# Attention and MLP kernel: a new order of the work, b1 turned on TensorE, w2 loaded in two parts

## The chip, the cores and the metric

The kernel runs on one NeuronCore of a Trainium2 chip. TensorE does the matmuls and writes to PSUM, VectorE and ScalarE do element-wise work, GpSimd and SyncE (SP) mostly issue DMAs; SP, ScalarE and GpSimd each have a DMA queue of their own. The engines run side by side, each takes its own list in order, and semaphores tie them. The metric is device time in microseconds (us); lower is better. In the profile PE is TensorE, PEld its weight load, DVE is VectorE, ACT is ScalarE, POOL is GpSimd.

## What is computed

```python
def _A_ref(x, wqkv, wo):          # S=2048, D=640, H=32 heads of 20, W=8, dil=2
    q, k, v = ...                 # x @ wqkv, split in heads
    idx = pos[:, None] - off[None, :]            # position minus 0, 2, .. 14
    logits = jnp.einsum("bhsd,bhswd->bhsw", q, kg) * scale   # masked where idx < 0
    attn = _softmax(logits, axis=-1)
    o = jnp.einsum("bhsw,bhswd->bhsd", attn, vg)
    return (...) @ wo

def _B_ref(x, w1, b1, w2, b2):    # F=1536
    h = _gelu(jnp.einsum("bsd,df->bsf", x, w1) + b1)
    return jnp.einsum("bsf,fd->bsd", h, w2) + b2

xn = _layernorm(x, axis=-1)
return x + _A_ref(xn, A_wqkv, A_wo) + _B_ref(xn, B_w1, B_b1, B_w2, B_b2)
```

Each position attends to eight positions, two apart, and an MLP stands beside the attention on the same normalised input. Data is bf16.

## The kernel before

The 2048 positions are cut in four chunks (n = 0 to 3) of 512, each of four blocks (bl) of 128. For a chunk the work is: statistics of x (`st`), rstd (`rs`, `rc`), normalised x (`xn`), its transpose into xnT (chunk 0: TensorE `tp` and copies `tc`; later chunks: DMA transposes `tc` on SP), projections to q, k, v held with features on the partitions (chunk 0 in pieces: matmuls `ga`, `gb`, `gd`, `ge`, `hj`, copies `gc`, `hc`; later `pj`, with copies `pc`), eight products q times shifted k on VectorE (`qk`), logits by TensorE (`lg`, four pieces wp = 0 to 3 for a chunk), max, subtract, exp, sum, reciprocal and weights (`m`, `mx`, `ex`, `ss`, `ri`, `at`), spread over the partitions by DMA (`xd` on SP, `xs` on ScalarE, `xw` both landed), eight weighted products with v (`av`), their sums (`ad`, `ot`). The MLP's first matmul is `f1` (12 tiles ft a chunk), its gelu on ScalarE `ge`. The output of a block is `o`: four steps over the gelu tiles with w2 and a fifth (`o..4`) over oT with wo, each matmul cut in "lo" (512 columns) and "hi" (128). Then come a copy (`oc`) and an accumulating DMA on GpSimd (`od`). A name is the kind followed by chunk and part: `lg23` is piece 3 of chunk 2, `f1010` is f1 of chunk 0, tile 10, `o104` the fifth step of chunk 1, block 0.

The order on TensorE, VectorE, ScalarE and SP is written out by hand: `ORDER` lists all pieces, and the program runs through it once, emitting each piece's instructions on its engines. So every engine's own order is the list cut down to its pieces. `make_plan` gives each piece its function; its costs and due times do not enter the built program.

Projections, f1 and the pieces of chunk 0 share four PSUM buffers (`acc`); a buffer is free again when ScalarE has copied it out (`hc`, `pc`, `ge`). The logits have one PSUM tile (tag L), which before the first chunk serves as target of ten idle matmuls; the output has one pair of banks (psO).

The logits matmuls sum over the 20 lanes of each head with a matrix of zeros and ones, 32 columns wide, so that four 32-column tiles of the array are in use, one for each block j:

```python
nc.tensor.matmul(L[j * H : (j + 1) * H, 2 * wp : 2 * wp + 2, :], lhsT=head_of[:],
                 rhs=prod[:, :, t, j * P : (j + 1) * P], ...)
```

The bias b1 (1536 numbers) is needed with features on the partitions, as b1T (128 x 12), the bias of every gelu. It is loaded as 12 rows of 128 into `b1_rt` (16 rows, zeroed by GpSimd at line 335) by SP at line 354, sixth in its queue; a DMA transpose at line 360 turns it into `b1_t`, and VectorE copies that to b1T (`b1`, line 589). Line 349 is the one x load on ScalarE's queue, line 364 (`ld`) loads w2.

Of the kernel before, what the change touches and what calls it, by code (L numbers as in the profile page):

```python
# [13 lines left out]
BF16 = mybir.dt.bfloat16  # L14
F32 = mybir.dt.float32
PE, VE, SE, DQ, GQ = "pe", "ve", "se", "dq", "gq"
# [46 lines left out]
S, D, F, H, W, DIL = 2048, 640, 1536, 32, 8, 2  # L63
P = 128
DH = D // H
PAD = (W - 1) * DIL
KT, FT = D // P, F // P
# [8 lines left out]
MW = 16  # L76
# [5 lines left out]


ORDER = """
pad01 pad02 st00a st00 sm rs00 me nm rc00 sq xn00a xn00b tp00a tp00b tc00a rs01 ga tc00b rc01 xn01 gb2 tp01 gb3
tc01a tc01b gb4 gd gc0 ge st03a hj101 gc4 st02a gc1 st02 hj100 st03 hc101 rs02 hj102 rs03 rc02 xn02 hj202 rc03 hc102
xn03 tp02 hc202 hj200 st10a tc02 st13a hc100 st13 tp03 hj201 tc03 st12a st11a hj112 st12 hc201 hj111 st10 hc200 st11
hj011 hc111 st21a st20a hc112 hj110 st22a hc011 st21 rs1 hj012 st20 hc110 hj010 st23a hc012 st22 hj211 rc1 hc010
st23 xn13 qk011 f101 hc211 tc13 hj212 pad11 qk031 xn10 f108 hc212 f102 b1 qk021 ge08 tc10 hj210 qk001 ge01 f100 xn11
qk020 f104 hc210 tc11 ge00 f105 qk010 ge02 xn12 f1010 qk030 ge04 tc12 f109 ge010 qk000 f1011 st33a ge011 ld lg00  # L90
st32a rs2 lg01 lg02 lg03 ge09 pj104 mk m0 pj114 ge05 mx0 pc104 pj102 pc114 st31a ex0 pj112 st30a rc2 st33 pj111 st32
pj101 ss0 pc111 pj110 pc101 ri0 pc112 pj103 pad12 xn22 st30 pj100 at0 pc102 tc22 pc103 pj113 st31 pc100 pc110 f103
pc113 qk110 f107 xd0 ge03 f110 qk131 xs0 f106 qk121 ge10 f113 qk101 pj121 ge13 xw0 ge06 f112 qk100 pc121 xn23 f115
qk120 ge12 tc23 f118 xn21 qk130 ge07 pj123 qk111 o020 xn20 tc21 o021 ge18 lg10 rs3 lg11 av030 pj122 tc20 av000 o022
pc122 lg12 av001 lg13 pj120 av011 o023 pc120 ge15 pj124 av031 f111 rc3 pc124 av021 pj210 xn32 pad21 pj202 tc32 av010
pc123 pc210 pj212 ge11 av020 pj211 pc212 pc202 ad00 pj214 xn33 pc211 pj213 tc33 xn31 pj200 pc213 ad01 pc214 pj224
tc31 pj203 ad02 pj220 pc203 pc224 pj204 pc220 xp0 f1110 pc204 ot0 pc200 pj223 m1 pj201 pc223 xb0 o024 mx1 pc201 xn30
qk220 pj221 oc02 tc30 ex1 o000 qk231 o001 o002 qk210 o003 ss1 o004 ri1 pj313 oc00 pc221 at1 od00 pj301 pc313 o010
qk221 xd1 pc301 pad22 pj310 qk200 o011 pc310 pj303 qk201 o012 pc303 qk211 xs1 o013 pj300 xw1 qk230 o014 xl lg20 oc01
lg21 av110 pc300 o030 lg22 ge110 av130 lg23 pj311 m2 xp1 o031 xb1 mx2 f119 av101 ex2 o032 f117 av100 pj312 pc311 ss2  # L100
f138 pc312 od02 ge17 pj302 av120 o033 pc302 av111 f114 ge19 pj314 ad10 f121 pc314 ge38 f116 ge21 ri2 pad31 f1210 xp2
av121 o034 ge210 xb2 av131 f1111 oc03 at2 pj304 ge111 pj321 ad11 pc304 pj322 pc321 xb3 ge16 pj222 ge14 qk310 pc322
od01 o100 xs2 od03 o101 ad12 o102 pj320 f128 ot1 f130 ge28 qk320 pc320 pj323 xd2 qk300 o103 o104 qk301 f129 oc10
qk331 pc323 o110 xw2 f126 qk321 o111 ge26 qk311 pc222 o112 pj324 qk330 f127 pc324 lg30 lg31 av211 o113 lg32 av230
o114 av220 lg33 oc11 f125 m3 od11 o120 ge25 av210 o121 o122 av231 o123 o124 mx3 f123 av221 oc12 od12 o130 av200 o131
ge23 od10 ge29 o132 ad21 ex3 o133 o134 ge27 ss3 f1211 f122 av201 f124 ge22 ad20 ge211 f131 ge30 oc13 f120 f132 ge20
ad22 ge24 f1310 f1311 ge310 ge31 ri3 o210 ge311 o211 at3 o212 ot2 xs3 xd3 o213 f134 o214 f135 oc21 pad32 od21 o220
xw3 ge35 o221 o222 av300 o223 o224 av320 f137 oc22 av310 od22 o230 av331 o231 o232 av301 o233 o234 av330 f136 av321
oc23 od23 o200 ad31 o201 ge32 ge34 f133 ge37 f139 ge33 av311 ge36 o202 ge39 o203 ad30 o204 o330 oc20 o310 ad32 od20
o300 od13 o301 o311 ot3 o312 o302 o303 o313 o304 o314 oc30 od30 o320 oc31 o321 od31 o322 o323 o324 o331 oc32 o332  # L110
od32 o333 o334 ohi oclo ochi
""".split()


def make_plan(fns, offsets={}):

    pl = Plan(offsets)
# [6 lines left out]
    def f(kind, *a):  # L124
        return lambda: fns[kind](*a)

    def turned(n, pair=None):
        if n:
            return [f"tc{n}{bl}" for bl in range(BPC)]
        every = ["tc00a", "tc00b", "tc01a", "tc01b", "tc02", "tc03"]  # L130
        return every if pair is None else every[4 * pair : 4 + 4 * pair]
# [5 lines left out]
            f"hc{which}1{g}" for g in range(len(COLS))  # L137
        ]

    pl.add("b1", VE, 0.1, -90, [], f("b1"), after=24.3)  # L140
    for n in range(NCH):
        base = n * PERIOD
        prev = base - PERIOD
# [51 lines left out]
        if n == 0:  # L195
# [11 lines left out]
            for which, buf, land in ((0, q, wq), (1, k, wk), (2, v, wv)):  # L207
                for pair in range(0 if which else 1, 2):
                    for g, (a, b) in enumerate(COLS):
                        ps = ("acc", "gp", which, pair, g)  # L210
                        nm = pl.add(f"hj{which}{pair}{g}", PE, 0.55 * (b - a), -50 + which // 2, turned(0, pair), f("gp", which, pair, a, b), [xnT, ps], land)
# [12 lines left out]
        L = ("L", n)  # L224
# [62 lines left out]
def kernel(  # L287
# [16 lines left out]
    nc = tc.nc  # L304
# [6 lines left out]
    consts = ctx.enter_context(tc.tile_pool(name="consts", bufs=1))  # L311
    wts = ctx.enter_context(tc.tile_pool(name="wts", bufs=1))
    psA = ctx.enter_context(tc.tile_pool(name="psA", bufs=4, space=bass.MemoryType.PSUM))
    psL = ctx.enter_context(tc.tile_pool(name="psL", bufs=1, space=bass.MemoryType.PSUM))
# [16 lines left out]
    w2_sb = wts.tile([P, FT, D], BF16, name="w2_sb")  # L331
    wo2 = wts.tile([P, KT, D], BF16, name="wo2")
    b1_rt = consts.tile([MW, P], BF16, name="b1_rt")
    b1_t = consts.tile([P, MW], BF16, name="b1_t")
    nc.gpsimd.memset(b1_rt[:], 0.0)
    b2bc = consts.tile([P, D], BF16, name="b2bc")
    wqkv_v = A_wqkv.rearrange("(t p) n -> p t n", p=P)
# [3 lines left out]
    def load_x(b0, b1):  # L341
        nc.sync.dma_start(x_sb[:, b0:b1, :], x_nb[:, b0:b1, :])  # L342

    def load_w(s):
        nc.sync.dma_start(wqkv[s][:], wqkv_v[:, :, s * D : (s + 1) * D])  # L345

    load_x(0, 1)
    nc.vector.memset(x_sb[:, 1, 0:16], 0.0)
    nc.scalar.dma_start(x_sb[:, 1, :], x_nb[:, 1, :])
    load_w(0)  # L350
    load_w(1)
    load_x(2, BPC)
    load_w(2)
    nc.sync.dma_start(b1_rt[0:FT, :], B_b1.rearrange("(t p) -> t p", p=P))  # L354
    load_x(BPC, 2 * BPC)
    load_x(2 * BPC, NCH * BPC)
    for c in range(2):
        cs = slice(c * F // 2, (c + 1) * F // 2)
        nc.sync.dma_start(w1_sb[:, :, cs], w1_v[:, :, cs])
    nc.sync.dma_start_transpose(b1_t[:], b1_rt[:])  # L360


    def do_ld():
        nc.sync.dma_start(w2_sb[:], B_w2.rearrange("(t p) n -> p t n", p=P))
        nc.sync.dma_start(wo2[:], A_wo.rearrange("(p t) n -> p t n", t=KT))
        nc.sync.dma_start(b2bc[:], b2_bcast)


    ident = consts.tile([P, P], BF16, name="ident")
# [10 lines left out]
    b1T = consts.tile([P, FT], F32, name="b1T")  # L380
# [15 lines left out]
    tiles = {}  # L396
# [179 lines left out]
    def do_qk(n, wp, i):  # L576
# [8 lines left out]
            op=ALU.mult,  # L585
        )

    def do_b1():
        nc.vector.tensor_copy(b1T[:], b1_t[:, 0:FT])

    def do_lg(n, wp):
        L = get(("L", n), lambda: psL.tile([P, W, P], F32, tag="L", name="L"))
# [172 lines left out]
    with tc.manual_schedule(engines=engines):  # L765

        ones = nc.const_aps.tensor(1.0, [P, CH], BF16)
        idle = psL.tile([P, W, P], F32, tag="L", name="idle")
        for _ in range(WARM):
            nc.tensor.matmul(idle[:, 0:BPC, :], lhsT=ones[:, 0:P], rhs=ones, start=True, stop=True)  # L770
        pieces = make_plan(fns).by
        assert sorted(ORDER) == sorted(pieces)
        for name in ORDER:
            pieces[name]["fn"]()
# [30 lines left out]
```

## Time and profile before

| | |
|---|---|
| median of 6 runs (lowest, highest) | 214.41 us (214.18, 215.57) |
| profiled execution | 214.09 us |
| its span, first to last instruction | 212.1 us |
| granted TensorE clock | 1.00 in all of the span's slices |
| TensorE matmul, VectorE, ScalarE busy | 97%, 82%, 53% |
| HBM read and written | 10.0 MB and 7.5 MB |

The page gives busy times by engine, the chain of work that ended last, groups of instructions by line, and DMA issues. Matmul durations overlap (a 512-column matmul is shown with 0.38 us, and the next starts 0.22 us after it), so TensorE's time is read from starts. In the timeline each row is start (us from the span's start), busy us, engine, line, operation, output and inputs, count, and in brackets the idle time before it and what ended it.

| row of the page | what it is |
|---|---|
| L697 hps 234 records, L507 pps 73 + 71 + 74, L728 lo 184 + 77 | the 512-column matmuls (some records are missing; weight loads are all there) |
| L602 L x320, 10.2 us busy | the logits |
| L708 hT x48, 31.2 us busy; 7 table loads there, 9.0 us | gelu |
| L581 x32 and L675 x32, 45.4 and 45.8 us | the products qk and av |

### The profile page before, as it was taken

To read this page: it belongs to the slowest core of one execution; us is meant where nothing else is said; L and a number is where in the kernel's file an instruction comes from. 1 tells how busy PE (TensorE), PEld (TensorE's weight loads), DVE (VectorE), ACT (ScalarE), POOL (GpSimd) and SP (SyncE) were. 2 spreads that over 40 slices of the span, in tenths; PEclk is the share of its full clock that TensorE was granted. 3 is DMA by queue.
4 is the path that set the end of the run, shared out by engine and by line. 5 is a ranking of instruction groups with operands and counts; after the bars stand their busy time and mean duration, and the time that the engine had idled before them with its cause. 6 is when DMAs were issued, how large, how long until landed. Compare 5 with 4: busy or idle time off the path is not lost.

```text
span 212.1 us, 3641 instructions
## 1 busy us (share of the span) xinstructions
PE 205.7 (97%) x1510; PEld 117.7 (56%) x1534; DVE 173.5 (82%) x178; ACT 112.7 (53%) x194; POOL 19.8 (9%) x37
## 2 busy tenths in 40 slices
PE   7999989999999999999999999999999999999994
PEld 2999636554465555555645554555554555555552
DVE  3588996889979999997899999969999819998001
ACT  5676797995866856551576452312287321341210
POOL 2000000000000002110120240101101011101120
PEclk9999999999999999999999999999999999999999
DMA  6999827928220173776653699701121381222053
GB/s 219 365 362 372 74 39 184 387 50 183 62 49 0 31 186 33 126 119 133 156 72 61 216 144 188 142 4 15 20 31 8 45 199 19 30 29 31 0 65 62
DMA packets 24104, 23.93 MB, mean 113 GB/s; under 512 B 9112, under 2 KB 21912, under 8 KB 24088
## 3 DMA queue, kind: packets, MB, share of 16 engines
q1 hardware_dynamic: 17064, 14.69, 26.5%
q0 software_dynamic: 4144, 4.92, 17.9%
q10 hardware_dynamic: 2880, 4.10, 6.4%
q8 instruction: 12, 0.20, 0.4%
q14 instruction: 4, 0.03, 0.1%
HBM read 10.00 MB, written 7.54 MB: 83 GB/s over the span
## 4 chain that ended last, share of the span: by engine, by line
PE 85%; DMA 6%; DVE 3%; SPq 2%; issue 1%; ACT 1%; ACTq 0%
PE lo L728 27%; PE hps L697 23%; PE pps L507 23%; PE hi L730 8%; DMA x_sb<-in_A_x_dram 6%; PE L L602 5%; DVE stats L407 2%; DVE prod L581 1%; SPq L345 1%; SPq L342 1%; ACT L708 1%; SPq L354 0%; ACT hT L708 0%; DVE mv L409 0%; DVE osb L758 0%
## 5 line engine op out<-in xcount | busy, mean ns | idle before, releaser
L697 PE MATMUL hps<-xnT,w_sb 128*128 128x512 bf16 x234 | 55.6, 379 | 1.1 <-ACT hT L708 0.7
L675 DVE TENSOR_TENSOR pv<-vT,ax 128x2560 bf16<-128x2560 bf16 x32 | 45.8, 1483 | 10.6 <-DMA ax<-attn 7.5
L728 PE MATMUL lo<-w_sb,hT 128*128 128x512 bf16 x184 | 52.9, 379 | 0.1
L581 DVE TENSOR_TENSOR prod<-qT,kT 128x2560 bf16<-128x2560 bf16 x32 | 45.4, 1484 | 0.8 <-ACT kT L566 0.8
L730 PE MATMUL hi<-w_sb,hT 128*128 128x128 bf16 x192 | 40.3, 219 | 0.5 <-issue 0.2
L708 ACT ACTIVATE hT<-hps,b1T 128x512 bf16<-128x512 f32 x48 | 31.2, 688 | 17.2 <-PE hps L697 15.2
L697 PEld LDWEIGHTS <-w_sb 128*128 128x128 bf16 x240 | 22.8, 98 | 27.1 <-issue 1.4
L684 DVE TENSOR_TENSOR pv<-pv 128x5120 bf16<-128x5120 bf16 x12 | 33.8, 2822 | 0.2
L735 ACT CAST osb<-lo 128x512 bf16<-128x512 f32 x15 | 8.8, 586 | 46.8 <-PE hi L730 25.5
L728 PEld LDWEIGHTS <-hT 128*128 128x128 bf16 x192 | 18.7, 98 | 22.4 <-issue 0.4
L741 POOL DMA_DIRECT2D out_dram<-osb x15 | 13.0, 866 | 103.3 <-ACT osb L736 87.7
L728 PE MATMUL lo<-wo,oT 128*128 128x512 bf16 x77 | 22.5, 379 | 0.0
L730 PEld LDWEIGHTS <-hT 128*128 128x128 bf16 x192 | 18.4, 98 | 2.8
L507 PE MATMUL pps<-xnT,wq_sb 128*128 128x512 bf16 x73 | 18.4, 379 | 0.1
L507 PE MATMUL pps<-xnT,wv_sb 128*128 128x512 bf16 x71 | 18.0, 380 | 0.2
L507 PE MATMUL pps<-xnT,wk_sb 128*128 128x512 bf16 x74 | 17.8, 379 | 0.0
L407 DVE BATCH_NORM_STATS2 stats<-x_sb 128x6 f32<-128x320 bf16 x30 | 13.0, 470 | 5.4 <-DMA x_sb<-in_A_x_dram 5.4
L730 PE MATMUL hi<-wo,oT 128*128 128x128 bf16 x80 | 16.9, 219 | 0.2
L488 POOL DMA_DIRECT2D out_dram<-b2bc x4 | 5.7, 1652 | 83.7 <-DMA out_dram<-x_sb 83.7
L728 PEld LDWEIGHTS <-oT 128*128 128x128 bf16 x80 | 7.8, 98 | 9.5 <-issue 0.2
L507 PEld LDWEIGHTS <-wk_sb 128*128 128x128 bf16 x75 | 8.6, 118 | 7.3 <-issue 0.2
L507 PEld LDWEIGHTS <-wq_sb 128*128 128x128 bf16 x75 | 8.6, 118 | 7.3 <-issue 0.2
(73 smaller groups left out, 199.9 us busy)
## 6 DMA issues: line engine op xcount, KB each, us to landing
out_dram<-osb POOLq DMA_DIRECT2D x15, 160.0 KB, 3.4
ax<-attn SPq DMA_DIRECT2D x8, 256.0 KB, 4.3
ax<-attn ACTq DMA_DIRECT2D x8, 256.0 KB, 6.0
w_sb<-in_B_w_dram SPq DMA_DIRECT2D x2, 960.0 KB, 13.8
w_sb<-in_B_w_dram SPq DMA_DIRECT2D x1, 1920.0 KB, 8.8
out_dram<-b2bc POOLq DMA_DIRECT2D x3, 640.0 KB, 6.9
x_sb<-in_A_x_dram SPq DMA_DIRECT2D x1, 1280.0 KB, 13.2
out_dram<-x_sb ACTq DMA_DIRECT2D x1, 1120.0 KB, 4.6
```

The source lines that it names most:

```text
L407: nc.vector.bn_stats(stats[:, i, :], x_sb[:, b, i * (D // 2) : (i + 1) * (D // 2)])
L507: nc.tensor.matmul(ps[:], lhsT=wqkv_p[which][:, ti, to, :], rhs=xnT[:, ti, :], start=(ti == 0), stop=(ti == KT - 1),)
L581: nc.vector.tensor_tensor(out=prod[:, i, :, :], in0=qkv_tile(n, 0)[:], in1=qkv_tile(n, 1)[:, :, off : off + CH], op=ALU.mult,)
L602: nc.tensor.matmul(L[j * H : (j + 1) * H, 2 * wp : 2 * wp + 2, :], lhsT=head_of[:], rhs=prod[:, :, t, j * P : (j + 1) * P], start=(t == 0 ...
L675: nc.vector.tensor_tensor(out=pv[:, i, :, :].rearrange("p t (j c) -> p t j c", j=BPC), in0=qkv_tile(n, 2)[:, :, off : off + CH].rearrange( ...
L684: nc.vector.tensor_tensor(out=ta[:], in0=ta[:], in1=tb[:], op=ALU.add)
L697: nc.tensor.matmul(ps[:], lhsT=w1_sb[:, ti, ft * P : (ft + 1) * P], rhs=tiles["xnT", n][:, ti, :], start=(ti == 0), stop=(ti == KT - 1),)
L708: nc.scalar.activation(hT[:], tiles["hps", n, ft][:], ACT.Gelu_apprx_tanh, bias=b1T[:, ft : ft + 1], scale=1.0)
L728: nc.tensor.matmul(lo[:], lhsT=lhs, rhs=rhs[:, 0:CH], start=first, stop=last)
L730: nc.tensor.matmul(hi[:, 0 : D - CH], lhsT=lhs, rhs=rhs[:, CH:D], start=first, stop=last)
L735: nc.scalar.copy(osb[:, 0:CH], tiles["lo", n, bl][:])
L741: nc.gpsimd.dma_start(rows, tiles["osb", n, bl][:], accum_op=ALU.add)
```

## The change

`ORDER` is another list over the same pieces (and one more, `tb`). Its beginning, the surroundings of the logits of chunks 1 to 3 and of `ot3`:

```diff
-pad01 pad02 st00a st00 sm rs00 me nm rc00 sq xn00a xn00b tp00a tp00b tc00a rs01 ga tc00b rc01 xn01 gb2 tp01 gb3
-tc01a tc01b gb4 gd gc0 ge st03a hj101 gc4 st02a gc1 st02 hj100 st03 hc101 rs02 hj102 rs03 rc02 xn02 hj202 rc03 hc102
...
-st23 xn13 qk011 f101 hc211 tc13 hj212 pad11 qk031 xn10 f108 hc212 f102 b1 qk021 ge08 tc10 hj210 qk001 ge01 f100 xn11
-qk020 f104 hc210 tc11 ge00 f105 qk010 ge02 xn12 f1010 qk030 ge04 tc12 f109 ge010 qk000 f1011 st33a ge011 ld lg00
-st32a rs2 lg01 lg02 lg03 ge09 pj104 mk m0 pj114 ge05 mx0 pc104 pj102 pc114 st31a ex0 pj112 st30a rc2 st33 pj111 st32
...
-qk120 ge12 tc23 f118 xn21 qk130 ge07 pj123 qk111 o020 xn20 tc21 o021 ge18 lg10 rs3 lg11 av030 pj122 tc20 av000 o022
-pc122 lg12 av001 lg13 pj120 av011 o023 pc120 ge15 pj124 av031 f111 rc3 pc124 av021 pj210 xn32 pad21 pj202 tc32 av010
...
-qk221 xd1 pc301 pad22 pj310 qk200 o011 pc310 pj303 qk201 o012 pc303 qk211 xs1 o013 pj300 xw1 qk230 o014 xl lg20 oc01
-lg21 av110 pc300 o030 lg22 ge110 av130 lg23 pj311 m2 xp1 o031 xb1 mx2 f119 av101 ex2 o032 f117 av100 pj312 pc311 ss2
...
-qk331 pc323 o110 xw2 f126 qk321 o111 ge26 qk311 pc222 o112 pj324 qk330 f127 pc324 lg30 lg31 av211 o113 lg32 av230
-o114 av220 lg33 oc11 f125 m3 od11 o120 ge25 av210 o121 o122 av231 o123 o124 mx3 f123 av221 oc12 od12 o130 av200 o131
...
-o300 od13 o301 o311 ot3 o312 o302 o303 o313 o304 o314 oc30 od30 o320 oc31 o321 od31 o322 o323 o324 o331 oc32 o332
+pad01 pad02 st00a st00 sm rs00 me nm rc00 sq xn00a xn00b tp00a tp00b tc00a rs01 tb ga tc00b rc01 xn01 gb2 b1 tp01
+gb3 tc01a tc01b gb4 gd gc0 ge st03a hj101 gc4 st03 st02a rs03 hj102 st02 hc101 hj100 rs02 hc102 rc02 rc03 gc1 hj200
+xn03 xn02 hc100 st11a tp03 tp02 st13a tc03 hj201 st11 tc02 st10a hj202 hc200 st12a hj012 st10 hj010 st13 hc012 hc202
+st12 hj111 hc010 hc201 hj011 rs1 hc111 rc1 st21a hj110 hc011 st22a st22 hj112 hc110 st20a hj212 st33a hc112 f102
+xn10 qk031 hc212 f100 xn13 tc10 qk001 ge02 f109 qk020 hj210 pad11 tc13 ge09 hj211 qk010 xn11 f108 hc211 qk000 ge00
+f101 tc11 qk011 f105 ge01 ge08 qk021 f104 xn12 f1011 tc12 ge04 qk030 f1010 ge011 st23a st21 lg00 ge010 st20 ld lg01
+ge05 st23 lg02 lg03 st31a rs2 pj114 mk m0 pj102 pc114 st32a st30a pj110 pc102 mx0 hc210 pj111 pc110 st32 ex0 pj101
...
+pad21 f106 ge12 qk110 xs0 f115 ge06 qk131 xw0 f110 rs3 qk101 o020 tc22 xn20 o021 ge15 lg10 lg11 av011 lg12 pc121
+tc20 lg13 ge10 rc3 pj120 av000 o022 pc120 av031 xn32 o023 pj122 tc32 av021 f111 pc122 m1 xn30 pj124 ge11 av030 tc30
...
+lg20 oc01 lg21 av130 pc303 lg22 pc224 lg23 av100 o030 f138 av110 o031 od00 ge38 av111 pj312 o032 pc301 m2 ge110 f117
...
+pj321 pc320 qk311 xd2 xs2 o110 pc324 qk301 o111 pc321 o112 qk310 f120 qk300 f126 xw2 f130 ge26 qk320 f127 xl lg30
+ge27 lg31 av201 lg32 lg33 o113 m3 o114 av211 f1311 oc11 av200 od11 o120 o121 od10 av221 o122 av230 o123 o124 av220
...
+o204 ad32 o310 oc20 o311 o300 ot3 o301 o302 o303 o304 o312 oc30 o313 od30 o320 od20 o321 o322 o323 o314 o324 oc31
```

The other parts:

```diff
-    pl.add("b1", VE, 0.1, -90, [], f("b1"), after=24.3)
+    pl.add("tb", PE, 0.1, -99, ["tp00b"], f("tb"))
+    pl.add("b1", VE, 0.1, -90, ["tb"], f("b1"))
...
-    b1_t = consts.tile([P, MW], BF16, name="b1_t")
...
     nc.scalar.dma_start(x_sb[:, 1, :], x_nb[:, 1, :])
+    nc.scalar.dma_start(b1_rt[0:FT, :], B_b1.rearrange("(t p) -> t p", p=P))
     load_w(0)
...
-    nc.sync.dma_start(b1_rt[0:FT, :], B_b1.rearrange("(t p) -> t p", p=P))
...
-    nc.sync.dma_start_transpose(b1_t[:], b1_rt[:])
...
-        nc.sync.dma_start(w2_sb[:], B_w2.rearrange("(t p) n -> p t n", p=P))
+        w2_v = B_w2.rearrange("(t p) n -> p t n", p=P)
+        for c in range(2):
+            ts = slice(c * FT // 2, (c + 1) * FT // 2)
+            nc.sync.dma_start(w2_sb[:, ts, :], w2_v[:, ts, :])
...
+    def do_tb():
+        tiles["tb"] = psL.tile([P, 2 * W * P], BF16, tag="L", name="tb")
+        nc.tensor.transpose(tiles["tb"][:, 0:MW], b1_rt[:], ident[0:MW, 0:MW])
+
     def do_b1():
-        nc.vector.tensor_copy(b1T[:], b1_t[:, 0:FT])
+        nc.vector.tensor_copy(b1T[:], tiles["tb"][:, 0:FT])
```

On TensorE the new order also takes most of the pieces of k, q and one of v of chunk 0 before the first f1, and within the logits groups of chunks 1 to 3 only pieces of other engines stand.

More of the change, by code (lines that the diff above doesn't have):

```diff
@@ L84 @@
 ORDER = """
-pad01 pad02 st00a st00 sm rs00 me nm rc00 sq xn00a xn00b tp00a tp00b tc00a rs01 ga tc00b rc01 xn01 gb2 tp01 gb3
-tc01a tc01b gb4 gd gc0 ge st03a hj101 gc4 st02a gc1 st02 hj100 st03 hc101 rs02 hj102 rs03 rc02 xn02 hj202 rc03 hc102
-xn03 tp02 hc202 hj200 st10a tc02 st13a hc100 st13 tp03 hj201 tc03 st12a st11a hj112 st12 hc201 hj111 st10 hc200 st11
-hj011 hc111 st21a st20a hc112 hj110 st22a hc011 st21 rs1 hj012 st20 hc110 hj010 st23a hc012 st22 hj211 rc1 hc010
-st23 xn13 qk011 f101 hc211 tc13 hj212 pad11 qk031 xn10 f108 hc212 f102 b1 qk021 ge08 tc10 hj210 qk001 ge01 f100 xn11
@@ L90 @@
-qk020 f104 hc210 tc11 ge00 f105 qk010 ge02 xn12 f1010 qk030 ge04 tc12 f109 ge010 qk000 f1011 st33a ge011 ld lg00
-st32a rs2 lg01 lg02 lg03 ge09 pj104 mk m0 pj114 ge05 mx0 pc104 pj102 pc114 st31a ex0 pj112 st30a rc2 st33 pj111 st32
-pj101 ss0 pc111 pj110 pc101 ri0 pc112 pj103 pad12 xn22 st30 pj100 at0 pc102 tc22 pc103 pj113 st31 pc100 pc110 f103
-pc113 qk110 f107 xd0 ge03 f110 qk131 xs0 f106 qk121 ge10 f113 qk101 pj121 ge13 xw0 ge06 f112 qk100 pc121 xn23 f115
-qk120 ge12 tc23 f118 xn21 qk130 ge07 pj123 qk111 o020 xn20 tc21 o021 ge18 lg10 rs3 lg11 av030 pj122 tc20 av000 o022
@@ L95 @@
-pc122 lg12 av001 lg13 pj120 av011 o023 pc120 ge15 pj124 av031 f111 rc3 pc124 av021 pj210 xn32 pad21 pj202 tc32 av010
-pc123 pc210 pj212 ge11 av020 pj211 pc212 pc202 ad00 pj214 xn33 pc211 pj213 tc33 xn31 pj200 pc213 ad01 pc214 pj224
-tc31 pj203 ad02 pj220 pc203 pc224 pj204 pc220 xp0 f1110 pc204 ot0 pc200 pj223 m1 pj201 pc223 xb0 o024 mx1 pc201 xn30
-qk220 pj221 oc02 tc30 ex1 o000 qk231 o001 o002 qk210 o003 ss1 o004 ri1 pj313 oc00 pc221 at1 od00 pj301 pc313 o010
-qk221 xd1 pc301 pad22 pj310 qk200 o011 pc310 pj303 qk201 o012 pc303 qk211 xs1 o013 pj300 xw1 qk230 o014 xl lg20 oc01
@@ L100 @@
-lg21 av110 pc300 o030 lg22 ge110 av130 lg23 pj311 m2 xp1 o031 xb1 mx2 f119 av101 ex2 o032 f117 av100 pj312 pc311 ss2
-f138 pc312 od02 ge17 pj302 av120 o033 pc302 av111 f114 ge19 pj314 ad10 f121 pc314 ge38 f116 ge21 ri2 pad31 f1210 xp2
-av121 o034 ge210 xb2 av131 f1111 oc03 at2 pj304 ge111 pj321 ad11 pc304 pj322 pc321 xb3 ge16 pj222 ge14 qk310 pc322
-od01 o100 xs2 od03 o101 ad12 o102 pj320 f128 ot1 f130 ge28 qk320 pc320 pj323 xd2 qk300 o103 o104 qk301 f129 oc10
-qk331 pc323 o110 xw2 f126 qk321 o111 ge26 qk311 pc222 o112 pj324 qk330 f127 pc324 lg30 lg31 av211 o113 lg32 av230
@@ L105 @@
-o114 av220 lg33 oc11 f125 m3 od11 o120 ge25 av210 o121 o122 av231 o123 o124 mx3 f123 av221 oc12 od12 o130 av200 o131
[L106 to L109, printed above, removed]
@@ L110 @@
-o300 od13 o301 o311 ot3 o312 o302 o303 o313 o304 o314 oc30 od30 o320 oc31 o321 od31 o322 o323 o324 o331 oc32 o332
-od32 o333 o334 ohi oclo ochi
+pad01 pad02 st00a st00 sm rs00 me nm rc00 sq xn00a xn00b tp00a tp00b tc00a rs01 tb ga tc00b rc01 xn01 gb2 b1 tp01
+gb3 tc01a tc01b gb4 gd gc0 ge st03a hj101 gc4 st03 st02a rs03 hj102 st02 hc101 hj100 rs02 hc102 rc02 rc03 gc1 hj200
+xn03 xn02 hc100 st11a tp03 tp02 st13a tc03 hj201 st11 tc02 st10a hj202 hc200 st12a hj012 st10 hj010 st13 hc012 hc202
+st12 hj111 hc010 hc201 hj011 rs1 hc111 rc1 st21a hj110 hc011 st22a st22 hj112 hc110 st20a hj212 st33a hc112 f102
@@ new lines @@
+xn10 qk031 hc212 f100 xn13 tc10 qk001 ge02 f109 qk020 hj210 pad11 tc13 ge09 hj211 qk010 xn11 f108 hc211 qk000 ge00
+f101 tc11 qk011 f105 ge01 ge08 qk021 f104 xn12 f1011 tc12 ge04 qk030 f1010 ge011 st23a st21 lg00 ge010 st20 ld lg01
+ge05 st23 lg02 lg03 st31a rs2 pj114 mk m0 pj102 pc114 st32a st30a pj110 pc102 mx0 hc210 pj111 pc110 st32 ex0 pj101
+rc2 st31 st30 pj100 st33 pj112 ss0 pc100 pc101 pj104 xn21 ri0 pj103 tc21 pc104 at0 pc111 pj113 pc103 pc112 pj123
+pc113 xn23 qk120 f113 pc123 tc23 xn22 f103 qk111 pj121 ge03 qk121 f118 xd0 qk130 ge13 f107 ge18 f112 qk100 ge07
@@ new lines @@
+pad21 f106 ge12 qk110 xs0 f115 ge06 qk131 xw0 f110 rs3 qk101 o020 tc22 xn20 o021 ge15 lg10 lg11 av011 lg12 pc121
+tc20 lg13 ge10 rc3 pj120 av000 o022 pc120 av031 xn32 o023 pj122 tc32 av021 f111 pc122 m1 xn30 pj124 ge11 av030 tc30
+pad12 pj214 av020 pj204 pc214 pj203 pc204 av001 pj211 pc203 av010 pc124 pj202 xn33 mx1 pc211 pj210 tc33 xn31 ad01
+pj221 pc210 pc202 pj223 tc31 pj201 ad00 pj220 pc201 pc223 pj213 xp0 pj200 pc213 ad02 pc221 pj212 pc220 pc200 pj224
+pc212 ex1 xb0 ot0 pj310 f1110 qk231 pc310 o024 qk220 pj300 oc02 ss1 pad31 od02 o000 o001 qk200 o002 o003 ri1 o004
@@ new lines @@
+at1 pj313 qk201 xd1 oc00 o010 pc313 qk211 pc300 pj301 xs1 qk210 o011 o012 qk221 o013 xw1 pj303 qk230 o014 xp1 xb1
+lg20 oc01 lg21 av130 pc303 lg22 pc224 lg23 av100 o030 f138 av110 o031 od00 ge38 av111 pj312 o032 pc301 m2 ge110 f117
+pc312 av131 f116 av120 pj304 pj302 mx2 o033 pc302 av121 ge16 f121 ge17 ad11 f1111 xp2 f1210 ge21 xb2 ge111 o034
+ge210 av101 pad22 pc304 f119 ad10 pj311 pj222 pc311 xb3 oc03 pj314 ad12 ge19 od01 f114 od03 f125 ge14 pc222 ot1
+pj324 pad32 pc314 ex2 o100 qk331 pj322 qk321 o101 ge25 o102 ss2 o103 pj323 ri2 o104 qk330 pc323 pc322 pj320 at2 oc10
@@ new lines @@
+pj321 pc320 qk311 xd2 xs2 o110 pc324 qk301 o111 pc321 o112 qk310 f120 qk300 f126 xw2 f130 ge26 qk320 f127 xl lg30
+ge27 lg31 av201 lg32 lg33 o113 m3 o114 av211 f1311 oc11 av200 od11 o120 o121 od10 av221 o122 av230 o123 o124 av220
+f1211 oc12 mx3 od12 o130 av210 o131 ge20 ge30 f124 ex3 ad20 f123 o132 ge311 o133 av231 o134 ge24 ss3 f128 ge211 oc13
+f129 ad21 ge23 f122 ge29 ge28 f131 ge22 ri3 o210 at3 f135 ad22 o211 xd3 f134 f1310 ot2 o212 ge310 ge31 o213 xs3 o214
+xw3 f137 oc21 ge34 od21 o220 av311 o221 o222 av300 o223 av310 o224 f136 av321 oc22 od22 o230 av301 o231 od13 o232
@@ L112 @@
+av320 o233 av331 o234 av330 f132 oc23 od23 o200 ad31 o201 ge32 ge36 o202 ge37 f139 ad30 f133 ge39 ge35 o203 ge33
+o204 ad32 o310 oc20 o311 o300 ot3 o301 o302 o303 o304 o312 oc30 o313 od30 o320 od20 o321 o322 o323 o314 o324 oc31
+od31 o330 oc32 o331 od32 o332 o333 o334 ohi oclo ochi
 """.split()
```

## The prediction

> **What bounds the kernel now.** I read the page's busy times and its chain of waits first,
>
> ```profile
> PE 205.7 (97%) x1510; PEld 117.7 (56%) x1534; DVE 173.5 (82%) x178; ACT 112.7 (53%) x194; POOL 19.8 (9%) x37
> ...
> PE 85%; DMA 6%; DVE 3%; SPq 2%; issue 1%; ACT 1%; ACTq 0%
> ```
>
> and from the table of waits (us in total, times, longest):
>
> ```profile
> PEld L602 <- issue: 2.4, 8, 0.4
> ...
> PE hps L697 <- ACT hT L708: 0.7, 1, 0.7
> ```
>
> TensorE is busy 97% of the span and makes 85% of the chain, so the question is how much of its time is not matmul work. Steps from one matmul's start to the next, in the timeline: 0.216 us for 512 columns (5 take 1.08), 0.109 for 256, 0.056 for 128. From the first q matmul at 6.03 the kernel issues 737 of 512 columns (225 projections, 240 of the first MLP matmul, 272 "lo"), 125 of 256, 50 + 15 + 272 of 128, and 320 logits matmuls: 159.2 + 13.6 + 18.9 + 8.7 (320 x 0.0272, below) = 200.4. The last one ends its step at 209.20, 203.2 after 6.03. So 2.8 us in all are not work, and no order can win more. The table of waits names the two parts of it: one wait on ScalarE's gelu, and eight entries into the logits matmuls. The timeline (start, us, engine, line) at the first:
>
> ```profile
> 25.18 0.17 DVE L589 CAST b1T<-b_t 128x12 f32<-128x12 bf16 x1
> ...
> 25.42 1.28 ACT L708 ACT_TABLE_LOAD   x1 [0.91 <-DVE b1T L589]
> 25.51 1.25 PE L551 MATMUL gps<-xnT,wv_sb 128*128 128x256 bf16 x10
> ...
> 27.46 6.63 PE L697 MATMUL hps<-xnT,w_sb 128*128 128x512 bf16 x29 [0.69 <-ACT hT L708]
> ```
>
> The ten 256-column matmuls from 25.51 use 1.09, so the next (f100) could start at 26.60; it starts at 27.46: 0.86 lost. It needs one of four PSUM buffers, freed by the first gelu; that gelu's table load stood 0.91 behind b1T, which VectorE copied only at 25.18. TensorE's rows of the timeline at two of the logits pieces:
>
> ```profile
> 34.02 2.37 PE L602 MATMUL L<-prod,head_of 128*32 128x256 bf16 x80
> 36.32 0.84 PE L507 MATMUL pps<-xnT,wq_sb 128*128 128x512 bf16 x2
> ...
> 59.51 0.22 PE L730 MATMUL hi<-w_sb,hT 128*128 128x128 bf16 x1
> 59.66 1.28 PE L602 MATMUL L<-prod,head_of 128*32 128x256 bf16 x40
> 60.87 0.41 PE L507 MATMUL pps<-xnT,wv_sb 128*128 128x512 bf16 x1
> ```
>
> The logits' tile is 128x32, the others' 128x128. Entry: "hi" at 59.51 has a step of 0.056, the logits start 0.15 after it: 0.09 lost. Exit: 80 in one piece hold TensorE from 34.02 to 36.32 (2.30), 40 from 59.66 to 60.87 (1.21); so 0.0272 each and 0.12 over. A change of tile and back costs 0.21, and there are eight: 1.7. With the 0.86 and 0.2 left over (0.16 of it one late buffer at 109.5) that is the 2.8.
>
> **The change, part by part.**
>
> *Whole groups.* The old list has 1, 2, 2 and 3 separate pieces in the four chunks (pj122 and o022; o030; o113 and o114 stand between). In the new list only work of other engines stands inside a group. Eight changes become four: -4 x 0.21 = -0.84, on TensorE, which sets the end.
>
> *b1 early.* SP loses the b1 load (0.96 of issue at 3.42, below) and the DMA transpose (3.95 of issue at 12.30, landing 11.2 later at 23.5). ScalarE's queue gains the load behind x's second block. The lead-in's rows:
>
> ```profile
> 0.91 0.39 ACTq L349 DMA_DIRECT2D x_sb<-in_A_x_dram x1
> ...
> 3.42 0.96 SPq L354 DMA_DIRECT2D b_rt<-in_B_b_dram x1
> 3.62 0.74 ACT L415 ACTIVATE xn<-x_sb 128x640 bf16<-128x640 bf16 x1 [1.39 <-DMA x_sb<-in_A_x_dram]
> ...
> 7.34 0.29 DVE L468 COPY xnT<-tp 128x256 bf16<-128x256 bf16 x1 [0.56 <-PE tp L463]
> ```
>
> On ScalarE the issue runs from 1.30 for 0.39 to 0.96 and ends by 2.26; the next work waits for x until 3.62, so it is free (without that cover: up to 0.96); GpSimd's memset that the load waits for ends at 0.92. The other x load of this queue landed 2.7 after issue, so b1 should land near 4 to 5. TensorE's transpose "tb" stands between tp00b and ga: the fifth transpose's step ends at 5.83 and ga starts at 6.03, on a copy. No row has a 16-row transpose. Below: it fits in the 0.2, zero; above: a full change of tile, 0.21, plus 0.06 of work, less the 0.2 of cover if it is lost. I take 0.06, one step of the 128-column transposes it is nearest to. The range keeps 0 to 0.27. Behind tb on TensorE stands everything, so a late b1 is paid in full (a rival below). VectorE's copy moves from 25.18 to between xn01 (ends 6.78) and the xnT copy at 7.34: 0.17 in a hole of 0.56, free; without the hole it would cost its 0.17. tb borrows the logits' bank, free again 25 before lg00.
>
> The Trainium skill, "TensorEngine Tiling (Array Packing)", section Key Properties, speaks against tb: a change of tiling mode drains TensorE, and a 16-row operand could be taken as one. The eight logits entries show such a cost at 0.21 a pair; by the rule the sum for tb would be 0.21, by the transposes' row 0.06.
>
> On SP, x's later loads are issued 1 us sooner, but the 16 DMA engines already move 362 to 372 GB/s there and w1's load waits for an earlier landing until 6.25: zero, 0.2 of gain at the most. After 12.2 SP next does something at 22.83, when ScalarE has the first xn; the transpose's 3.95 lay in that gap: zero.
>
> *The first gelu.* With b1T done by 7, the table load would follow the last cast at 24.5 and gelu would end 0.9 sooner: the 0.86 is gone, unless the new order makes another wait. Laid out: k, q and one v piece run first, f102 from 21.2 to 22.2, f100 to 23.3, f109 to 24.4, hj210, hj211, f108, f101. ScalarE, one cast ending near 21.2, then xn10 (0.83 a step), a cast 0.3, xn13 0.83, table 1.28, gelu 0.69: ends 25.1, and its buffer is wanted at 25.5 by hj211. Then a pad copy, a gelu, xn11 and a cast (0.16, 0.6, 0.83, 0.57): 27.3, wanted at 27.7 by f101. So 0.2 to 0.4 in hand; then 0.1 twice (f104, f1010). I take -0.86, bounds -0.86 and 0 (an equal wait elsewhere).
>
> *The rest of the list.* Laid end to end by the same steps, buffers come free within 0.2 of need at some twelve places, against nineteen in the old list, whose one late buffer cost 0.16. I take +0.25 for new waits (between none and the largest sum, nearer to what the old list shows), bounds -0.16 (none, and the old one gone) and +1.0 (twelve of 0.08). The last logits end some 4 earlier (old 145.5, new near 141.6, of which 2.4 was work standing between pieces), the softmax and oT of the last chunk follow; old oT ends at 195.7, 2 before its first use. The new first use is 3 earlier: covered.
>
> *w2 in two.* One more SP issue (0.58 at 32.77). Old w2 lands at 41.6, first use 57.94; the transposes behind it wait for xn, so 16 us cover it: zero. Without cover the price is the 0.58.
>
> **Sum.** -0.84 - 0.86 + 0.06 + 0.25 = -1.39. The profiled execution has 214.09 (span 212.1 and 2.0 around it): 212.7. The median of the six runs is 0.32 above that execution: 213.0. Less than 0.3% (0.64 us) is what a measurement of this kernel can't tell from no change; the bound is at 213.77.
>
> **Rivals.**
>
> *The gelu wait only moves.* ScalarE's load of casts, xn and gelu between 21 and 33 is no smaller, and three of four buffers turn over while one waits for a late cast (hc210). For it: reserves of 0.1 to 0.4 above. Against: the 0.91 that ScalarE stood idle is time it now has. Then only the groups count: 214.41 - 0.84 + 0.1 = 213.7, between 213.4 and 213.9.
>
> *Slower: whole groups wait for their last product.* TensorE takes its list in order; with nothing between the pieces, it stands at the group until VectorE has the products. By VectorE's steps (1.40 a product) the last product of chunk 1 ends near 58.5 and the group's turn is at 59.0; of chunk 3 139.2 against 139.7. Old reserves: 0.4 and 1.0. If VectorE is late at three groups by 0.9 each (its waits for the ax loads were up to 5.4 once), that is +2.7, which also pushes the rest: 214.41 - 1.4 + 2.7 = 215.7. It decides from 1.4 of total lateness, and is slower from 2.0. Against: VectorE has 18% idle, and products come first in its list.
>
> *Slower: b1 is late.* If tb's operand came as in the old queue, where data behind the weights landed near 11.4, ga would start 5.4 late: about 218. Against: the x load on ScalarE's queue overtook wq.
>
> *It does nothing:* the four changes of tile cost only what overlaps anyway. Against: 1.21 and 2.30 are starts, not busy times. 214.2 to 214.6.
>
> **How the numbers follow.** Forecast 0.66 (own range 212.3 to 213.7), the wait that moves 0.16, late products 0.10, late b1 0.04, nothing 0.04. The range for 8 in 10 goes from 212.3 (214.41 - 0.84 - 0.86 - 0.16 - 0.2) to 214.1, which takes in the wait that moves. Faster: 0.62 of the forecast and half of the first rival, 0.70. Within 0.3%: 0.04, 0.08, 0.04 and 0.01, 0.17. Slower: 0.13.
>
> **What would show it.** Four entries of L602 "issue" in the waits, near 1.2; no wait of hps on ScalarE near 26 to 28; ga at 6.03 to 6.1; the last "hi" near 207.8. A wait of L602 on VectorE, or of tb on a DMA, would make the prediction wrong.

## The result and the profile after

The changed kernel has a median of 212.46 us (212.21 to 214.48, 15 runs) against 214.36 (213.96 to 216.28, 34 runs): a ratio of 0.9915, interval 0.990 to 0.993, so 1.9 us faster and outside the 0.3% that can't be told from no change. Its profiled execution has 212.45 (span 210.5), that of before 214.09 (212.1). The forecast was 213.0, the range 212.3 to 214.1.

The page of the changed kernel, busy times and the chain of waits by engine:

```profile
PE 205.6 (98%) x1511; PEld 118.8 (56%) x1535; DVE 173.4 (82%) x178; ACT 111.9 (53%) x193; POOL 19.8 (9%) x37
...
PE 98%; issue 1%; DVE 0%
```

TensorE's busy time hardly moved (205.7 to 205.6); what left is time between matmuls. The chain now follows TensorE for 98% instead of 85%: the transfers and VectorE steps that stood in it are gone. The table of waits of the changed kernel (us in total, times, longest):

```profile
PEld L608 <- issue: 1.0, 3, 0.4
...
PEld L608 <- DVE prod L583: 0.4, 1, 0.4
```

L608 is the logits line now. Four entries of 0.4 instead of eight; one is put down to a product, but it is no longer than the other three. No wait of TensorE on a gelu stands in the table any more. The first gelu in the timeline of the changed kernel (start, us, engine, line):

```profile
21.56 9.90 DVE L583 TENSOR_TENSOR prod<-qT,kT 128x2560 bf16<-128x2560 bf16 x7 [0.44 <-ACT kT L563]
...
23.38 1.28 ACT L714 ACT_TABLE_LOAD   x1
...
24.67 2.35 PE L553 MATMUL gps<-xnT,wv_sb 128*128 128x256 bf16 x20
24.67 0.69 ACT L714 ACTIVATE hT<-hps,b1T 128x512 bf16<-128x512 f32 x1
...
26.86 3.40 PE L703 MATMUL hps<-xnT,w_sb 128*128 128x512 bf16 x15
```

Twenty 256-column matmuls from 24.67 should hand over 20 x 0.109 = 2.19 later, at 26.86, and they do: nothing is lost. The gelu ends at 25.36 (25.1 was laid out), before TensorE wants its buffer.

To see where the time went, TensorE's records are cut at the starts of three matmuls in the profiled execution. What stands ahead of the first q matmul is the lead-in. A is from the first q matmul to the last logits matmul of chunk 0, B from there to the last matmul of all; the first column plus A plus B is that last start (to 0.01, by rounding), and from it to the end of the execution is 4.94 in the kernels before and after, 4.77 to 5.39 in the others. The median is of all runs, not of the profiled one.

| kernel | first q matmul | A | B | last matmul | median |
|---|---|---|---|---|---|
| before | 6.03 | 30.09 | 173.04 | 209.15 | 214.36 |
| changed | 6.08 | 29.43 | 171.99 | 207.51 | 212.46 |
| old order, early b1 | 6.14 | 29.80 | 173.09 | 209.03 | 214.26 |
| old order, early products and b1 | 6.34 | 29.21 | 173.30 | 208.85 | 213.71 |
| old order, whole groups | 6.46 | 29.77 | 172.23 | 208.46 | 213.60 |
| old order, all three | 7.71 | 29.21 | 172.28 | 209.20 | 212.89 |
| new order, split groups | 6.34 | 29.17 | 174.29 | 209.80 | 214.76 |
| new order, old b1 | 6.15 | 30.06 | 171.99 | 208.20 | 214.27 |
| changed, six more turns | 7.30 | 30.55 | 171.99 | 209.84 | 214.81 (one run) |
| changed, turn first | 6.22 | 29.17 | 171.99 | 207.39 | 212.34 |
| changed, w2 in one load | 6.16 | 29.21 | 171.99 | 207.37 | 212.42 |

A is 29.2 wherever nothing stands in the way. The changed kernel's profiled execution lies 0.26 above that, for a reason told at the end. A wait inside A that ends at a fixed time takes up a late lead-in: in the old order with whole groups the first q matmul comes 0.43 later than before and the wait for the gelu is 0.57 instead of 0.86, so its A is smaller without any gain. The ratios below are taken against the kernel before on the same chip, whose medians there were 214.26 (experiments 1 to 4), 214.31 (5, 6, 7 and 9) and 214.24 (8).

### The profile page after: what moved, and what is told of

It is laid out like the page before. It is cut to its first block, busy times and chain, and to the rows that moved or that the text cites. A ratio compares the mean times of both kernels' runs of the same rounds, so it can differ in the third digit from the quotient of the medians.

```text
span 210.5 us, 3645 instructions
## 1 busy us (share of the span) xinstructions
PE 205.6 (98%) x1511; PEld 118.8 (56%) x1535; DVE 173.4 (82%) x178; ACT 111.9 (53%) x193; POOL 19.8 (9%) x37
## 4 chain that ended last, share of the span: by engine, by line
PE 98%; issue 1%; DVE 0%
PE lo L734 27%; PE hps L703 24%; PE pps L509 23%; PE hi L736 8%; PE gps L553 6%; PE L L608 4%; PE idle L776 2%; PE gps L522 1%; PE tp L465 1%; DVE osb L764 0%; PE tb L592 0%
## 5 line engine op out<-in xcount | busy, mean ns | idle before, releaser
L734 PE MATMUL lo<-wo,oT 128*128 128x512 bf16 x74 | 21.9, 379 | 0.0
L747 POOL DMA_DIRECT2D out_dram<-osb x15 | 13.6, 904 | 86.2 <-ACT osb L742 80.1
L568 ACT CAST qT<-pps 128x512 bf16<-128x512 f32 x15 | 8.7, 590 | 8.8 <-PE pps L509 8.8
```

Of the source, the lines that this page charges most:

```text
L734: nc.tensor.matmul(lo[:], lhsT=lhs, rhs=rhs[:, 0:CH], start=first, stop=last)
L747: nc.gpsimd.dma_start(rows, tiles["osb", n, bl][:], accum_op=ALU.add)
```

## The experiments

**1. Whole groups alone.** The old list with nothing of TensorE inside the groups; the rest is the kernel before.

```diff
-lg11 av030 pj122 tc20 av000 o022 pc122 lg12 av001 lg13
+lg11 av030 tc20 av000 lg12 av001 lg13 pj122 o022 pc122
...
-pc300 o030 lg22 ge110 av130 lg23
+pc300 lg22 ge110 av130 lg23 o030
...
-av211 o113 lg32 av230 o114 av220 lg33
+av211 lg32 av230 av220 lg33 o113 o114
```

> The kernel before with pj122, o022, o030, o113 and o114 moved behind their logits groups, so that there are four; b1 and w2 as before. My theory: -0.84, about 213.5, ratio 0.996. If whole groups wait for their last product: the group of chunk 1, whose reserve was 0.4, or of chunk 3 shows a wait on VectorE, and the gain is smaller than 0.5 or gone.

Measured: 213.60 (213.15 to 213.89, 8 runs), ratio 0.9974 (0.9963 to 0.9985). B falls from 173.04 to 172.23, by 0.81, and the table of waits of this kernel has the four entries:

```profile
PEld L601 <- issue: 1.4, 4, 0.4
```

No entry waits for VectorE. The median falls by 0.66; the profiled execution's first q matmul was late. So the groups bring their 0.84, here without any of the rest. The four changes themselves are worth a little more: five k matmuls from 108.31 hand over at 109.67, 0.28 later than their 1.08 would have it, just behind ScalarE's copy of kT (the wait of experiment 5), where before loses 0.16 at the same place. Without the 0.12 between them B falls by 0.93, 0.23 for each change of tile and back.

**2. The same from the other side.** The changed kernel with the groups split again at four places.

```diff
-lg10 lg11 av011 lg12
+lg10 lg11 av011 o022 lg12
...
-lg21 av130 pc303 lg22 pc224 lg23 av100 o030
+lg21 av130 pc303 o030 lg22 pc224 lg23 av100
...
-av201 lg32 lg33 o113 m3 o114
+av201 o113 lg32 o114 lg33 m3
```

> The changed kernel with o022, o030, o113 and o114 put back between the logits pieces of chunks 1, 2 and 3, so that there are eight groups again; nothing else. If a change of tile costs 0.21 us (my theory): four more make 0.84, about 213.3 against 212.46 of the changed kernel. If whole groups are worth nothing: 212.4 to 212.6.

Measured: 214.76 (214.54 to 217.22, 12 runs), ratio 1.0043 (1.0023 to 1.0062): slower than before by 0.5 us. B is 174.29, 2.29 over the changed kernel, and 0.84 explains only part. Waits of this kernel:

```profile
DVE m L620 <- PE L L607: 2.8, 1, 2.8
...
PEld L733 <- DVE oT L695: 1.6, 1, 1.6
```

VectorE's timeline of this kernel, and chunk 2's oT in that of the changed kernel:

```profile
145.10 1.23 DVE L620 TENSOR_REDUCE m<-L 128x128 f32<-128x1024 f32 x1 [2.76 <-PE L L607]
...
169.22 1.49 DVE L695 TENSOR_TENSOR oT<-pv 128x2560 bf16<-128x2560 bf16 x1
```

```profile
166.17 1.49 DVE L696 TENSOR_TENSOR oT<-pv 128x2560 bf16<-128x2560 bf16 x1
```

TensorE's timeline of this kernel:

```profile
169.31 0.22 PE L735 MATMUL hi<-w_sb,hT 128*128 128x128 bf16 x1
170.77 0.39 PE L733 MATMUL lo<-wo,oT 128*128 128x512 bf16 x1 [1.24 <-DVE oT L695]
```

The last logits matmul of chunk 3 starts at 144.78 instead of 141.73; VectorE reaches the max of chunk 3 at its place in the list and stands there for 2.8. Everything behind it is late, chunk 2's oT starts at 169.22 instead of 166.17, and TensorE waits 1.41 for it. What is left of the 2.29 is 0.88, 0.22 for each of the four changes of tile and back. The new list without other moves only fits whole groups.

**3. Early b1 alone.** The old list with `tb` behind `rs01` and `b1` in the lead-in, and the changed kernel's code for both; w2 in one load.

```diff
-rs01 ga tc00b rc01 xn01 gb2 tp01
+rs01 tb ga tc00b rc01 xn01 gb2 b1 tp01
...
-f102 b1 qk021
+f102 qk021
```

> The order of before, with b1 loaded on ScalarE's queue and turned by TensorE as in the change; w2 in one load. If the gelu's wait for b1T was a loss by itself (my theory): f100 starts where the ten matmuls before it end, TensorE's last matmul 0.86 - 0.06 = 0.8 us earlier, about 213.55 against 214.36, ratio 0.996. If the wait only moves to the next PSUM buffers: no hole at 26.6 but others before 34, the logits of chunk 0 at 34.0 as before, 214.2 to 214.4. Eight entries into the logits in both.

Measured: 214.26 (213.91 to 216.07, 11 runs), ratio 1.0015 (0.9998 to 1.0033): no gain at all. Timeline of this kernel, TensorE and VectorE:

```profile
26.10 1.26 PE L549 MATMUL gps<-xnT,wv_sb 128*128 128x256 bf16 x10
27.19 6.64 PE L699 MATMUL hps<-xnT,w_sb 128*128 128x512 bf16 x29
33.85 2.37 PE L604 MATMUL L<-prod,head_of 128*32 128x256 bf16 x80
```

```profile
22.53 11.26 DVE L579 TENSOR_TENSOR prod<-qT,kT 128x2560 bf16<-128x2560 bf16 x8
```

The hole at the first gelu is gone (10 x 0.109 = 1.09, and the next follows at once), yet the logits begin at 33.85 against 34.02. The first of them needs the product that VectorE makes last (`qk000`), and that ends at 22.53 + 11.26 = 33.79. TensorE comes to the logits and waits, 0.09 here; wv had landed 1.0 later than before in this execution and had already cost 0.39 at 11.95. Had it not, the wait should have been longer and the logits no sooner; no run shows that. In the profile of before the limit could be read: VectorE's timeline,

```profile
22.42 2.85 DVE L581 TENSOR_TENSOR prod<-qT,kT 128x2560 bf16<-128x2560 bf16 x2
...
25.26 8.49 DVE L581 TENSOR_TENSOR prod<-qT,kT 128x2560 bf16<-128x2560 bf16 x6
```

ends the last product at 33.75, 0.27 ahead of the logits at 34.02. Of the 0.86 no more than that was to be had in the old order.

**4. The new order with b1 by the old way.** `tb` and `b1` out of the lead-in, `b1` behind `qk001`, load and DMA transpose as before; w2 in two loads.

```diff
-qk001 ge02
+qk001 b1 ge02
```

> The changed kernel's order and its two w2 loads, but b1 loaded on SP and turned by the DMA transpose, its copy behind the first two products on VectorE as before. If the early b1 is needed in the new order too (my theory): the copy runs near 24.4, the table load 1.1 later than 23.4, and TensorE waits for the first gelu at hj211, by 0.7 to 0.9: about 213.2. If the new order alone removes the wait: at most 0.2 more than 212.46, and no wait of TensorE on ScalarE before 34.

Measured: 214.27 (213.59 to 216.52, 12 runs), ratio 1.0005 (0.9983 to 1.0027). The table of waits of this kernel:

```profile
PE gps L553 <- ACT hT L710: 0.7, 1, 0.7
```

It is the wait of before at another matmul (`hj211`, 0.86 late), and A is 30.06 instead of 29.2. So the new order needs the early b1, and loses all of the 0.86 without it. The median is 1.8 above the changed kernel's: five of the twelve runs lie at 213.6 to 213.75, which the profile (213.59) explains, six at 214.25 to 214.8 and one at 216.5, which it doesn't. The spans of those six are 0.1 to 0.8 longer than the five's, so that a part of their lateness lies outside the span; its cause stays open.

**5. Old order, early b1, and the products sooner.** As 3, with four statistics pieces of chunk 2 moved from ahead of the products to behind them, as the new list has it.

```diff
-st21 rs1 hj012 st20 hc110 hj010 st23a hc012 st22 hj211 rc1 hc010 st23
+st21 rs1 hj012 hc110 hj010 hc012 hj211 rc1 hc010
...
-qk000 f1011 st33a
+qk000 f1011 st22 st20 st23a st23 st33a
```

> As e1 (old order, early b1, w2 in one load), and four statistics of x (st20, st22, st23, st23a) moved behind the products of chunk 0 on VectorE. If e1 gained nothing because TensorE then waited for VectorE's last product of chunk 0 (my theory now): products start at 21.4 in place of 22.5, the logits of chunk 0 start at 33.1 to 33.3, and the time falls by 0.6 to 0.9 against before, 213.4 to 213.7. If e1's loss lay elsewhere (b1's load on ScalarE's queue that delays the weights, the extra turn on TensorE): no more than 0.3 sooner than e1's 214.26.

Measured: 213.71 (213.59 to 216.56, 12 runs), 0.60 under before by the medians; the ratio 0.9987 has an interval of 0.9952 to 1.0023, which doesn't settle it. The profile does. VectorE's timeline of this kernel:

```profile
21.81 11.31 DVE L579 TENSOR_TENSOR prod<-qT,kT 128x2560 bf16<-128x2560 bf16 x8 [1.56 <-ACT qT L559]
```

The products start at 21.81 instead of 22.53, now as soon as ScalarE has copied q, and A falls to 29.21, all of the 0.86. B grew by 0.26, since TensorE waits 0.42 at 109.0 for ScalarE's copy of kT, where before waits 0.16:

```profile
PE hps L699 <- ACT kT L564: 0.3, 1, 0.3
```

**6. All three in the old order.** 5 and the edit of 1 together.

> As e8, and the logits groups of chunks 1 to 3 made whole as in e3. If the three causes are all there is in the change (my theory): 0.84 less than e8, 212.5 to 212.9, within 0.3 of the changed kernel. If the rest of the new list is worth something by itself: 213.0 or more.

Measured: 212.89 (212.68 to 214.42, 12 runs), ratio 0.9928 (0.9904 to 0.9953). A is 29.21 and B 172.28; B's 0.3 over the changed kernel is the same wait for kT, 0.33 at 109.9. Three edits to the old list thus give all but 0.4 of the change, and one wait that the new list doesn't have is most of that. The profiled execution was the longest of the runs (214.42): wq landed at 7.67, and the first q matmul was 1.6 late.

**7. Six more turns of b1**, each between two pieces in the packed stretch from 22 to 30, into a part of the tile that nothing reads.

```diff
-f102 xn10 qk031 hc212 f100 xn13
+f102 tb1 xn10 qk031 hc212 f100 tb2 xn13
...
+    def do_tbx(i):
+        nc.tensor.transpose(tiles["tb"][:, 32 * i : 32 * i + MW], b1_rt[:], ident[0:MW, 0:MW])
```

> The changed kernel with the turn of b1 on TensorE done six times more, one behind each of f102, f100, f109, hj210, hj211 and f108, where matmuls stand back to back; the results go to free columns of the same tile and are not used. If a 16-row operand is a change of tile that drains the array (the rule weighed in the prediction): steps grow by 0.21 to 0.27 each, 1.3 to 1.6 in all, unless ScalarE's reserves hide some behind. If it is an ordinary transpose: 0.06 to 0.1 each, 0.3 to 0.6 in all.

Measured: 214.81 in one run. TensorE's timeline of this kernel and its waits:

```profile
22.42 1.24 PE L708 MATMUL hps<-xnT,w_sb 128*128 128x512 bf16 x5
23.59 0.18 PE L597 MATMUL tb<-ident,b_rt 16*128 16x16 bf16 x1
23.71 1.25 PE L708 MATMUL hps<-xnT,w_sb 128*128 128x512 bf16 x5
```

```profile
PEld L597 <- issue: 2.1, 6, 0.4
```

Five 512-column matmuls and one turn hold TensorE from 22.42 to 23.71, 1.29 instead of 1.08: 0.21. A is 30.55, 1.35 above 29.2, so 0.22 for each turn. That is the price of a change of tile and back, not of a short transpose. The Trainium skill, "TensorEngine Tiling (Array Packing)", section Key Properties, says that a change of tiling mode drains TensorE. The 0.21 agrees with it, and the 0.06 of the transposes' row doesn't; that TensorE drains is not itself seen in the trace. The rest of this execution's lateness is the lead-in: wq landed at 7.25.

**8. The turn ahead of xn's transposes.**

```diff
-xn00a xn00b tp00a tp00b tc00a rs01 tb ga
+xn00a xn00b tb tp00a tp00b tc00a rs01 ga
```

> The changed kernel with one edit: b1's turn (tb) stands ahead of the five transposes of xn in TensorE's list instead of behind them, and nothing is left out of the computation. In the changed kernel's profiled execution b_rt landed at 4.40 and the first transpose of xn began near 5.2, so the turn fits into TensorE's idle time there. Theory (tb sticks out by 0.055 us because it stands between the last transpose and the first q matmul): the first q matmul begins at 6.03 instead of 6.08 where wq has landed by then, and the median is 212.4, within 0.3% of the changed kernel's 212.46. Rival (a move of the first use of b_rt ahead of xn's transposes makes the lead-in wait for a late b_rt, as in the execution with six more turns, where it landed 0.7 later): the transposes of xn start after tb, the first q matmul begins 0.3 to 0.7 later, median 212.8 to 213.2.

Measured: 212.34 (212.28 to 212.68, 6 runs), ratio 0.9909 (0.9878 to 0.9940). The 0.12 under the changed kernel is less than can be told. The first q matmul came at 6.22, not at 6.03: the turn pushed xn's transposes back by 0.1 instead, and x had landed 0.1 later. Nothing waited for b1, which landed at 4.62. (In the execution with six more turns it landed at 6.52, 2.1 later than in the changed kernel's and not 0.7.) The theory's median came, its first q matmul didn't; there is nothing to win at this place.

**9. w2 in one load again**, the rest as changed.

> The changed kernel with w2 in one load. My theory: w2 lands 15 us or more before its first use, so 212.4 to 212.6, the same as the changed kernel. Rival: the issue that goes frees SP for the transposes behind it; then up to 0.6 sooner, and a row of TensorE that waited for xnT would show it.

Measured: 212.42 (212.35 to 213.84, 8 runs), ratio 0.9912 (0.9882 to 0.9941); B is 171.99 in both. The split load is worth nothing that can be told. With 8 this is the best that was found, and neither beats the changed kernel by what can be told.

## Why the prediction was right, and where it wasn't

*Whole groups, -0.84:* right, a little low. 0.81 in experiment 1, 0.93 there without the longer wait for kT, and 0.88 left over in 2 once the wait is taken off; the rival that the changes of tile cost nothing falls.

*The first gelu, -0.86:* the size is right, the reason was half. A fell by 0.92 once the 0.26 for slow first matmuls (last section) is taken off (30.09 to 29.17), and experiment 4 gives 0.86 back. But the step asked only whether ScalarE would be done in time. Experiment 3 shows that b1T done by 7 brings nothing in the old order, because the next limit, VectorE's last product at 33.75, left only 0.27 of the 0.86 to be had. The new list starts the products 0.86 earlier (22.42 to 21.56) by putting statistics of chunk 2 behind them, and 5 shows that this and the early b1 together are what wins. In the prediction that move was not a term, so that the whole 0.86 came was luck on this side. The rival "the wait only moves" was thus true of the early b1 alone, with VectorE in the part that it gave to ScalarE.

*tb, +0.06:* the size came, but 0.06 was taken from the wrong row. The turn costs 0.21 to 0.22 in a packed stretch (7), as the rule had it, and the hole of 0.2 ahead of the first q matmul hid most or all of it. The first q matmul starts 0.05 later than before, but wq also landed 0.10 later (5.99 against 5.89), so 0.05 is the most that tb can have cost there. In experiments 2, 3, 5, 6, 7 and 9 the first q matmul waited for wq or for xnT's copy, and tb cost nothing. The bounds, 0 to 0.27, held both.

*New waits, +0.25:* too high, the mis-sized term. Two new waits of 0.02 each, at 93.5 and 111.6, and the old 0.16 at 109.5 gone: -0.12, near the lower bound. Some twelve places were laid out with 0.2 or less in hand; in the profile TensorE lost time at two.

*SP's queue, ScalarE's issue, VectorE's copy, w2 at zero:* right. The later x loads landed at 13.2 and 18.1 and the two w1 loads at 20.8 and 23.3, as before; b1 landed at 4.41; 9 has w2.

*Late products:* no. The last product of chunk 1 ended at 58.67 and the group began at 59.06; of chunk 3 139.36 and 139.63. So the reserves were 0.4 and 0.3, thinner than the 0.5 laid out, but they were not used up. *Late b1:* not in the changed kernel's profiled execution; in 6 and 7 b1 landed at 6.09 and 6.52, `tb` waited 0.2 and 0.4 for it, and wq, later still in both, set the start. That it cost nothing there is luck.

*The sum.* -0.84 - 0.86 + 0.05 - 0.12 = -1.77, and +0.26 for slow first matmuls makes -1.51; measured -1.64. The steps of the two traces hold the 0.13: a change of tile and back costs 0.23 instead of 0.21, 0.08 for four, and before loses another 0.06 near 23.3, where TensorE waited for the second half of w1 (landed 23.30). The forecast's profiled time was 212.70 against 212.45. The other half of the 0.54 between 213.0 and 212.46 is the 0.32 that was added because before's profiled execution lay under its median; the changed kernel's lay on it (212.45 and 212.46), which is chance.

## What to carry to other kernels

When a stall is taken away, ask what every engine at the next meeting point is doing: the time won is the distance to the second limit, which stands in the profile of before as the slack between the last producer's end and its consumer's start. On a packed engine a hole is a resource: the same small operation cost at most 0.05 in a hole and 0.22 elsewhere. An order of work written out by hand is one piece: the same regrouping won 0.8 of B in the old list, and taking it out of the new one cost 2.3, because other engines' places in the list had been moved to suit it.

## What of the hardware had not been expected

The first matmuls ran at different speeds from one execution to the next. The first fifteen q matmuls in the timeline of the changed kernel and of experiment 8:

```profile
6.08 1.26 PE L522 MATMUL gps<-xnT,wq_sb 128*128 128x128 bf16 x15
```

```profile
6.22 1.00 PE L521 MATMUL gps<-xnT,wq_sb 128*128 128x128 bf16 x15
```

In the first the steps are 0.107 us until 6.60 and 0.056 after; in the second they are 0.056 throughout. The ten idle matmuls of 512 columns ahead of them had steps of 0.427 us to their end in eight of the eleven profiled executions, while in those of before and of experiment 4 the last step was already 0.22 (in experiment 1 it was 0.37). The slow q matmuls cost the changed kernel's execution 0.26. They are not of the change: the ten matmuls start at 0.78 in every execution, and experiments 2 and 9, with the same lead-in, don't have the five slow steps. The Trainium skill, "TensorE: Matmul & The Clock Gate", Part 1, says that TensorE runs at half clock until a window of activity has passed, and that this window runs free of the kernel's start, so that the moment varies. That fits. The profile's row of granted clock doesn't show it: it has 9 in all slices, although the slow steps fill most of the first slice of 5.3 us. Here the clock has to be read from the steps.

The lead-in varies by more than most of the terms argued about: wq landed between 5.9 and 7.7 in the profiled executions, and in six of the eleven the first q matmul followed it within 0.05. In a stream that is packed from there on each tenth is paid in full: A is 29.21 in experiment 6 with the first q matmul at 7.71, as in 9 with it at 6.16. The two latest landings of wq, 7.25 and 7.67, and of b1, 6.52 and 6.09, fell in the same two executions. Both are kernels that load b1 beside wq; of the three that don't, the latest wq came at 6.41. Whether b1's load now and then holds wq up was not tested.
